# Token pairs for w, output weights four rows per partition, the old state on VectorE and a new order of steps, in a fused linear-attention and gated-MLP kernel

**Chip, cores, metric.** One core of a Trainium2 chip. The metric is device time in microseconds (us), the median of several executions. The kernel before takes 211.56 us (median of 3 runs, 211.44 to 212.03).

## The reference

A linear attention with a decaying state gives x for each token, and a gated MLP with an RMS norm is applied to x. All inputs are float32.

```python
# r, k, v, w: [4 batches, 8 heads, 768 tokens, 48]; u: [8, 48]
for t in range(S):
    cur = einsum('bhd,bhe->bhde', u * k[t], v[t])
    y[t] = einsum('bhd,bhde->bhe', r[t], state + cur)
    state = w[t][..., None] * state + einsum('bhd,bhe->bhde', k[t], v[t])
x = y.transpose(0, 2, 1, 3).reshape(3072, 384)
xn = x / sqrt(mean(x * x) + 1e-6) * rms_g
out = (silu(xn @ w_gate) * (xn @ w_val)) @ w_out     # 384 -> 1536 -> 384
```

## The kernel before

The 768 tokens are cut into 6 superblocks of 128 tokens; a superblock has one chunk per batch, so 4 chunks. Steps are named `step.n.j`, n the superblock, j the chunk or the block of 128 MLP units. One long list, `ORDER`, gives the order of all steps, and each engine executes its own instructions in that order. Loads of r, k, v and w are issued by SyncE, loads of the weights by GpSimd, in between its arithmetic. For a superblock the kernel forms Ln of w, sums it over time with a triangular mask on TensorE, takes the exponentials, multiplies r and k by them, and forms scores, state and y; then the norm, gate, value, `h_mul` and the output matmul. A 512-token superblock has 12 gate and 12 value blocks of three matmuls.

```python
    W_PAIR = ()
    OLD_DVE = ()
...
    def load_w(n, j):                        # one tile [128, 2 * 384] holds two chunks
        ...
        if n in W_PAIR:                      # tokens 2g and 2g+1 in one partition: 384 B runs
            o = t.rearrange("p (h x) -> p h x", h=H)[PD * (j % 2):PD * (j % 2) + PD]
            src = src.rearrange("h (g i) d -> g h (i d)", i=2)
        else:                                # one token per partition: 192 B runs
            o = t.rearrange("p (b h d) -> p b h d", b=2, h=H)[:, j % 2]
            src = src.rearrange("h t d -> t h d")
...
    wg_sb = persist.tile([128, KC, DF], BF16)        # KC = 3, DF = 1536
    wv_sb = persist.tile([128, KC, DF], BF16)
    GV = (0, 4, 12)                                  # two loads each: columns 0-511, 512-1535

    def load_gv(g, h):
        cols = slice(GV[g] * 128, GV[g + 1] * 128)
        dst, s = ((wg_sb, moe_w_gate), (wv_sb, moe_w_val))[h]
        i = nc.gpsimd.dma_start(out=dst[:, :, cols], in_=s[:, cols].rearrange("(c p) f -> p c f", p=128)).ins
        ...
    def load_wo(g, _):                               # FG = 4
        i = nc.gpsimd.dma_start(
            out=wo_sb[:, g * FG:(g + 1) * FG, :],
            in_=moe_w_out[g * FG * 128:(g + 1) * FG * 128, :].rearrange("(c p) m -> p c m", p=128)).ins
...
    def st_mm(n, j):
        ps = bank["st", n, j] = psQ.tile([128, NP, 2 * D], FP32, name="ps_q")
        old = n > 0 and n not in OLD_DVE
        if old:                                      # adds the old state: identity matmul
            nc.tensor.matmul(ps.rearrange("p q x -> p (q x)"), lhsT=ident,
                             rhs=st[:, n % 2, j].rearrange("p q x -> p (q x)"), start=True, stop=False)
        ...
    def st_new(n, j):
        ...
        if n in OLD_DVE:
            nc.vector.tensor_tensor(out=ps, in0=ps, in1=st[:, n % 2, j], op=ALU.add)
        ...
    def fc_mm(ps, ws, n, f):                         # gate and value
        for c in range(KC):
            nc.tensor.matmul(ps, lhsT=ws[:, c, f * 128:(f + 1) * 128], rhs=xnt[n][:, c, :],
                             start=(c == 0), stop=(c == KC - 1))
```

The branches for `W_PAIR` and `OLD_DVE` are there already, with empty lists.

Of the kernel before, what the change touches and what calls it, by code (L numbers as in the profile page):

```python
# [9 lines left out]
FP32 = mybir.dt.float32  # L10
BF16 = mybir.dt.bfloat16
AF = mybir.ActivationFunctionType
# [13 lines left out]
load_w.0.0 load_v.0.0 load_w.0.1 load_k.0.0 load_r.0.0 ln.0.0 load_w.0.2 load_r.0.1 ln.0.1 cs_mm.0.0 load_k.0.1  # L26
cs_mm.0.1 exp_k.0.0 load_w.0.3 exp_r.0.0 k_mul.0.0 bonus_mul.0.0 exp_r.0.1 r_mul.0.0 load_r.0.2 exp_k.0.1 w_tot.0.0
cast_v.0.0 rk_pe.0.0 load_k.0.2 ln.0.2 r_mul.0.1 st_mm.0.0 rk_tr.0.0 cs_mm.0.2 load_w.1.0 st_new.0.0 bonus_mul.0.1
load_v.0.1 q_mm.0.0 k_mul.0.1 ln.0.3 w_tot.0.1 bonus_sum.0.0 rk_pe.0.1 load_k.0.3 exp_k.0.2 q_mask_e.0.0 exp_r.0.2
cs_mm.0.3 bonus_v.0.0 q_mask_o.0.0 rk_tr.0.1 load_r.0.3 k_mul.0.2 y_mm.0.0 bonus_mul.0.2 exp_k.0.3 load_w.1.1  # L30
r_mul.0.2 q_mm.0.1 exp_r.0.3 x_add.0.0 ln.1.0 rk_pe.0.2 load_v.0.2 bonus_sum.0.1 x_sq.0.0 q_mask_e.0.1 cast_v.0.1
load_v.0.3 bonus_v.0.1 w_tot.0.2 rk_tr.0.2 q_mask_o.0.1 cs_mm.1.0 load_w.1.2 k_mul.0.3 bonus_mul.0.3 q_mm.0.2
bonus_sum.0.2 load_k.1.0 r_mul.0.3 ln.1.1 q_mask_o.0.2 rk_pe.0.3 load_w.1.3 x_rstd.0.0 cast_v.0.2 y_mm.0.1 bonus_v.0.2
load_r.1.0 rk_tr.0.3 x_add.0.1 load_gv.0.0 load_r.1.1 q_mask_e.0.2 cast_v.0.3 xn_mul.0.0 load_gv.0.1 bonus_sum.0.3
q_mm.0.3 ln.1.2 bonus_v.0.3 y_mm.0.2 x_sq.0.1 q_mask_e.0.3 st_mm.0.1 exp_k.1.0 load_gv.1.1 w_tot.0.3 x_add.0.2
x_rstd.0.1 cs_mm.1.1 q_mask_o.0.3 exp_r.1.0 load_gv.1.0 x_sq.0.2 y_mm.0.3 exp_k.1.1 load_v.1.0 xn_pe.0.0 x_rstd.0.2
x_add.0.3 st_mm.0.2 st_new.0.1 xn_mul.0.1 x_sq.0.3 st_new.0.2 st_mm.0.3 cs_mm.1.2 x_rstd.0.3 xn_out.0.0 xn_mul.0.2
xn_pe.0.1 xn_mul.0.3 xn_pe.0.2 xn_out.0.1 ln.1.3 xn_pe.0.3 xn_out.0.2 exp_r.1.1 xn_out.0.3 exp_k.1.2 cs_mm.1.3
exp_r.1.2 k_mul.1.0 gate_mm.0.0 st_new.0.3 exp_k.1.3 exp_r.1.3 val_mm.0.0 silu.0.0 gate_mm.0.1 h_mul.0.0 val_mm.0.1
silu.0.1 gate_mm.0.2 h_mul.0.1 load_k.1.1 val_mm.0.2 silu.0.2 gate_mm.0.3 r_mul.1.0 bonus_mul.1.0 val_mm.0.3 silu.0.3  # L40
load_v.1.1 h_mul.0.2 rk_pe.1.0 gate_mm.0.4 h_mul.0.3 load_k.1.2 rk_tr.1.0 r_mul.1.1 val_mm.0.4 load_k.1.3 silu.0.4
bonus_sum.1.0 gate_mm.0.5 cast_v.1.0 h_mul.0.4 load_r.1.2 bonus_v.1.0 val_mm.0.5 silu.0.5 gate_mm.0.6 load_r.1.3
bonus_mul.1.1 h_mul.0.5 val_mm.0.6 k_mul.1.1 silu.0.6 load_w.2.0 gate_mm.0.7 cast_v.1.1 h_mul.0.6 load_v.1.2 st_mm.1.0
load_wo.1.0 k_mul.1.2 silu.0.7 val_mm.0.7 load_w.2.1 st_new.1.0 gate_mm.0.8 bonus_mul.1.2 k_mul.1.3 q_mm.1.0 silu.0.8
rk_pe.1.1 q_mask_e.1.0 val_mm.0.8 rk_tr.1.1 r_mul.1.2 gate_mm.0.9 load_wo.0.0 h_mul.0.7 q_copy_o.1.0 st_mm.1.1
load_wo.2.0 rk_pe.1.2 st_new.1.1 load_k.2.0 val_mm.0.9 rk_tr.1.2 bonus_mul.1.3 r_mul.1.3 q_mm.1.1 gate_mm.0.10
silu.0.9 h_mul.0.8 q_copy_o.1.1 rk_pe.1.3 q_mask_e.1.1 silu.0.10 val_mm.0.10 q_mask_o.1.0 bonus_sum.1.1 rk_tr.1.3
q_mm.1.2 q_mask_o.1.1 gate_mm.0.11 q_mask_e.1.2 q_copy_o.1.2 load_v.1.3 y_mm.1.0 bonus_sum.1.2 silu.0.11 q_mask_o.1.2
x_add.1.0 q_mm.1.3 ln.2.0 bonus_v.1.1 y_mm.1.1 h_mul.0.9 bonus_v.1.2 h_mul.0.10 val_mm.0.11 q_mask_e.1.3 cast_v.1.2
load_r.2.0 cs_mm.2.0 q_copy_o.1.3 h_mul.0.11 y_mm.1.2 x_sq.1.0 load_w.2.2 st_mm.1.2 x_add.1.1 o_mm.0.0 st_new.1.2  # L50
x_rstd.1.0 x_sq.1.1 load_r.2.1 exp_k.2.0 x_rstd.1.1 ln.2.1 load_k.2.1 k_mul.2.0 exp_r.2.0 q_mask_o.1.3 bonus_sum.1.3
o_mm.0.1 cast_v.1.3 load_r.2.2 o_out.0.0 xn_mul.1.0 bonus_v.1.3 w_tot.2.0 x_add.1.2 load_v.2.0 bonus_mul.2.0 x_sq.1.2
y_mm.1.3 load_v.2.1 o_out.0.1 st_mm.1.3 x_add.1.3 ln.2.2 cs_mm.2.1 load_w.2.3 st_new.1.3 o_mm.0.2 x_sq.1.3 x_rstd.1.2
exp_k.2.1 r_mul.2.0 load_k.2.2 xn_mul.1.1 x_rstd.1.3 k_mul.2.1 xn_mul.1.2 bonus_sum.2.0 out_dma.0.0 cs_mm.2.2
exp_r.2.1 cast_v.2.0 o_out.0.2 xn_pe.1.0 xn_pe.1.1 load_r.2.3 r_mul.2.1 bonus_mul.2.1 xn_pe.1.2 xn_mul.1.3 o_mm.0.3
xn_out.1.0 exp_r.2.2 load_k.2.3 xn_out.1.1 ln.2.3 rk_tr.2.0 xn_out.1.2 exp_k.2.2 w_tot.2.1 r_mul.2.2 cast_v.2.1
xn_pe.1.3 cs_mm.2.3 o_out.0.3 bonus_mul.2.2 xn_out.1.3 st_mm.2.0 load_v.2.2 exp_r.2.3 w_tot.2.2 st_mm.2.1 k_mul.2.2
load_k.3.0 exp_k.2.3 gate_mm.1.0 r_mul.2.3 w_tot.2.3 val_mm.1.0 load_r.3.0 silu.1.0 k_mul.2.3 bonus_mul.2.3
gate_mm.1.1 bonus_sum.2.1 rk_tr.2.1 val_mm.1.1 q_mm.2.0 silu.1.1 h_mul.1.0 gate_mm.1.2 load_r.3.1 bonus_v.2.0
h_mul.1.1 load_k.3.1 val_mm.1.2 silu.1.2 q_mask_e.2.0 gate_mm.1.3 h_mul.1.2 rk_tr.2.2 bonus_mul.3.0 val_mm.1.3  # L60
silu.1.3 st_new.2.0 gate_mm.1.4 q_copy_o.2.0 rk_tr.2.3 bonus_sum.2.2 val_mm.1.4 h_mul.1.3 silu.1.4 cast_v.2.2
gate_mm.1.5 h_mul.1.4 load_v.2.3 bonus_v.2.1 val_mm.1.5 st_new.2.1 silu.1.5 load_w.3.0 q_mask_o.2.0 gate_mm.1.6
h_mul.1.5 load_w.3.1 bonus_mul.3.1 val_mm.1.6 q_mm.2.1 load_r.3.2 gate_mm.1.7 q_copy_o.2.1 q_mask_e.2.1 load_k.3.2
st_mm.2.2 silu.1.6 q_mask_o.2.1 val_mm.1.7 silu.1.7 h_mul.1.6 load_k.3.3 y_mm.2.0 h_mul.1.7 gate_mm.1.8 out_dma.0.1
x_add.2.0 val_mm.1.8 st_new.2.2 x_sq.2.0 load_w.3.2 gate_mm.1.9 silu.1.8 x_rstd.2.0 val_mm.1.9 load_w.3.3 silu.1.9
h_mul.1.8 gate_mm.1.10 out_dma.0.2 xn_mul.2.0 h_mul.1.9 q_mm.2.2 load_r.3.3 silu.1.10 bonus_sum.2.3 q_mm.2.3
q_mask_e.2.2 q_copy_o.2.2 val_mm.1.10 load_r.4.0 q_copy_o.2.3 q_mask_o.2.2 gate_mm.1.11 out_dma.0.3 h_mul.1.10
cast_v.2.3 val_mm.1.11 q_mask_e.2.3 silu.1.11 load_k.4.0 q_mask_o.2.3 y_mm.2.1 ln.3.0 h_mul.1.11 bonus_v.2.2 st_mm.2.3
load_r.4.1 y_mm.2.2 x_add.2.1 bonus_v.2.3 o_mm.1.0 load_k.4.1 st_new.2.3 ln.3.1 load_v.3.0 x_add.2.2 x_sq.2.1
bonus_sum.3.0 x_sq.2.2 x_rstd.2.1 bonus_sum.3.1 cs_mm.3.0 xn_pe.2.0 y_mm.2.3 x_rstd.2.2 exp_r.3.0 xn_out.2.0 o_mm.1.1  # L70
xn_mul.2.1 r_mul.3.0 bonus_mul.3.2 exp_k.3.0 x_add.2.3 xn_mul.2.2 o_out.1.0 x_sq.2.3 k_mul.3.0 cs_mm.3.1 ln.3.2
w_tot.3.0 rk_tr.3.0 xn_pe.2.1 x_rstd.2.3 o_mm.1.2 exp_r.3.1 exp_k.3.1 r_mul.3.1 bonus_mul.3.3 ln.3.3 k_mul.3.1
load_k.4.2 o_out.1.1 w_tot.3.1 xn_out.2.1 xn_mul.2.3 load_r.4.2 cs_mm.3.2 bonus_sum.3.2 load_v.3.1 cs_mm.3.3 o_out.1.2
exp_k.3.2 xn_pe.2.2 bonus_mul.4.0 xn_pe.2.3 exp_r.3.2 load_k.4.3 o_mm.1.3 xn_out.2.2 exp_k.3.3 r_mul.3.2 exp_r.3.3
load_r.4.3 xn_out.2.3 w_tot.3.2 k_mul.3.2 load_v.3.2 bonus_mul.4.1 gate_mm.2.0 r_mul.3.3 w_tot.3.3 k_mul.3.3
val_mm.2.0 out_dma.1.0 silu.2.0 gate_mm.2.1 rk_tr.3.1 val_mm.2.1 q_mm.3.0 silu.2.1 h_mul.2.0 load_r.5.0 gate_mm.2.2
q_copy_o.3.0 bonus_sum.3.3 load_k.5.0 val_mm.2.2 h_mul.2.1 silu.2.2 bonus_mul.4.2 load_v.3.3 gate_mm.2.3 h_mul.2.2
rk_tr.3.2 val_mm.2.3 silu.2.3 gate_mm.2.4 h_mul.2.3 bonus_v.3.0 load_w.4.0 val_mm.2.4 q_mask_e.3.0 silu.2.4 rk_tr.3.3
cast_v.3.0 gate_mm.2.5 bonus_sum.4.0 h_mul.2.4 st_mm.3.0 bonus_mul.4.3 silu.2.5 val_mm.2.5 st_new.3.0 load_r.5.1
gate_mm.2.6 load_k.5.1 bonus_sum.4.1 val_mm.2.6 h_mul.2.5 silu.2.6 cast_v.3.1 gate_mm.2.7 load_w.4.1 o_out.1.3  # L80
h_mul.2.6 cast_v.3.2 st_mm.3.1 q_mask_o.3.0 silu.2.7 load_r.5.2 val_mm.2.7 st_new.3.1 bonus_v.3.1 gate_mm.2.8
out_dma.1.1 h_mul.2.7 cast_v.3.3 q_mm.3.1 load_w.4.2 st_mm.3.2 bonus_mul.5.0 q_copy_o.3.1 y_mm.3.0 st_new.3.2 silu.2.8
val_mm.2.8 load_r.5.3 x_add.3.0 gate_mm.2.9 load_k.5.2 q_mask_e.3.1 val_mm.2.9 bonus_v.3.2 load_v.4.0 silu.2.9
bonus_sum.4.2 st_mm.3.3 x_sq.3.0 h_mul.2.8 q_mask_o.3.1 gate_mm.2.10 load_w.4.3 h_mul.2.9 bonus_v.3.3 val_mm.2.10
# [44 lines left out]
def kernel(  # L129
# [46 lines left out]
    CAST_ACT = sel("00 01 02 03 10 11 12 13")  # L176
    EXPR_SB = sel("10 11 12 13")
    EXPK_SB = sel("10 11 12 13")
    W_PAIR = ()
    Q_PAIR = ()  # L180
    OLD_DVE = ()
    XOUT_ACT = sel("")
# [475 lines left out]
```

## Time and profile before

| | before |
|---|---|
| time, median | 211.56 us |
| TensorE busy | 194.5 us, 92% |
| first gate matmul | 29.31 us |
| val of block 1, superblock 1 | 70.56 us |
| from there to the end | 140.9 us |
| gate and value weight loads issued by GpSimd at | 19.32, 20.31, 21.88, 22.68 us |

The page's lines are shown in the prediction (timelines: start, duration, then in brackets the idle time before and what ended it). The first gate block, from the TensorE timeline (start, duration, then in brackets the idle time before and what ended it):

```profile
29.31 0.58 PE L546 MATMUL ps_a<-xnt,wg_sb 128*128 128x512 bf16 x1
30.12 0.63 PE L546 MATMUL ps_a<-xnt,wg_sb 128*128 128x512 bf16 x1 [0.22 <-issue]
```

In all profile lines PE is TensorE (PEld its weight loads), DVE VectorE, ACT ScalarE, POOL GpSimd, SP SyncE; a small q behind a name is the engine issuing something, L546 a line of the kernel, `out<-in` the tiles, x3 the number of instructions, and after q0 and q1 stand packets, MB and the share of the 16 DMA engines. Some matmul records are missing from every trace: this block has three matmuls and two records.

### The profile page before, as it was taken

How to read it: one execution, taken by the hardware profiler on the slowest of the kernel's cores; microseconds unless marked ns; L12 is line 12 of the kernel's file. 1: busy time of each engine (PE TensorE's matmuls, PEld its weight loads, DVE VectorE, ACT ScalarE, POOL GpSimd, SP SyncE). 2: the span in 40 equal slices, each digit the busy share in tenths (PEclk: the TensorE clock that was granted, in tenths of full speed). 3: DMA queues.
4: the chain of work that ended last, by engine and by line, in shares of the span. 5: the costliest groups of instructions: out<-in, count | busy, mean ns of one | idle time of the engine just before them, and what ended most of it. 6: DMA issues, size and time to landing. Idle time of an engine off the chain costs nothing.

```text
span 211.5 us, 4381 instructions
## 1 busy us (share of the span) xinstructions
PE 194.5 (92%) x1534; PEld 107.7 (51%) x1552; DVE 147.6 (70%) x295; ACT 138.1 (65%) x282; POOL 108.6 (51%) x167
## 2 busy tenths in 40 slices
PE   5687779998998799999999999999999999999993
PEld 2455434455664245665455565455655544544563
DVE  6498744899876688988689799667886755235411
ACT  3796994769796356997546998578858873225300
POOL 3498402869597593699697889473222520000000
PEclk9999999999999999999999999999999999999999
DMA  6999999899999999999999999992177030000122
GB/s 131 217 217 183 171 203 211 169 201 168 194 205 188 190 186 228 219 213 192 192 195 222 230 222 124 236 188 48 56 186 127 20 76 20 37 0 37 40 111 76
DMA packets 126878, 32.41 MB, mean 153 GB/s; under 512 B 120580, under 2 KB 126088, under 8 KB 126856
## 3 DMA queue, kind: packets, MB, share of 16 engines
q1 hardware_dynamic: 123664, 28.58, 67.9%
q0 software_dynamic: 3184, 3.54, 10.4%
q8 instruction: 12, 0.20, 0.4%
q14 instruction: 10, 0.08, 0.1%
q10 hardware_dynamic: 8, 0.00, 0.0%
HBM read 25.96 MB, written 4.72 MB: 145 GB/s over the span
## 4 chain that ended last, share of the span: by engine, by line
PE 68%; DMA 7%; SPq 7%; DVE 6%; ACT 5%; issue 3%; POOL 3%; ACTq 0%; DVEq 0%; POOLq 0%
PE ps_b L546 20%; PE ps_a L546 19%; PE ps_q L606 18%; SPq L208 4%; DMA kt<-in_k_dram 3%; DMA vt<-in_v_dram 3%; PE ps_q L443 2%; SPq L221 2%; DMA xnt<-xn 2%; DVE ht L564 2%; PE ps_q L491 2%; PE ps_q L488 1%; DVE rk L402 1%; ACT junk L501 1%; PE ps_b L375 1%
## 5 line engine op out<-in xcount | busy, mean ns | idle before, releaser
L564 DVE TENSOR_TENSOR ht<-ps_b,sg 128x512 bf16<-128x512 f32 x72 | 48.7, 688 | 25.8 <-PE ps_b L546 18.6
L195 ACT ACTIVATE sg<-ps_a 128x512 bf16<-128x512 f32 x72 | 42.6, 596 | 36.3 <-PE ps_a L546 34.9
L546 PE MATMUL ps_b<-xnt,wv_sb 128*128 128x512 bf16 x208 | 58.6, 384 | 2.7 <-DVE rk L402 1.5
L546 PE MATMUL ps_a<-xnt,wg_sb 128*128 128x512 bf16 x206 | 58.8, 385 | 1.2 <-DVE wcol L394 0.6
L606 PE MATMUL ps_q<-wo_sb,ht 128*128 128x384 bf16 (+1 forms) x300 | 49.9, 319 | 0.0
L408 POOL TENSOR_TENSOR ruk<-rt,kt 128x384 f32<-128x384 f32 x24 | 24.3, 1011 | 25.5 <-DMA rt<-in_r_dram 20.2
L606 PEld LDWEIGHTS <-ht 128*128 128x128 bf16 x300 | 28.4, 98 | 16.9
L546 PEld LDWEIGHTS <-wv_sb 128*128 128x128 bf16 x216 | 20.2, 99 | 25.1 <-issue 4.9
L546 PEld LDWEIGHTS <-wg_sb 128*128 128x128 bf16 x216 | 20.2, 99 | 24.2 <-issue 1.7
L409 POOL TENSOR_TENSOR ruk<-ruk,u_bc 128x384 f32<-128x384 f32 x24 | 24.1, 1005 | 1.9
L418 POOL TENSOR_TENSOR ydiag<-vt,diag 128x384 f32<-128x384 f32 x24 | 19.8, 830 | 3.7 <-DVE diag L413 2.9
L461 POOL TENSOR_SCALAR_AFFINE_SELECT qts<-qts 128x512 bf16<-128x512 bf16 x20 | 12.6, 635 | 14.2 <-ACT qts L454 14.2
L450 DVE TENSOR_TENSOR qts<-ps_q,mask_lt 128x512 bf16<-128x512 f32 x24 | 16.2, 683 | 3.8 <-issue 2.5
L496 DVE TENSOR_TENSOR xb<-ps_q,ydiag 128x384 f32<-128x384 f32 x24 | 13.3, 552 | 5.3 <-PE ps_q L491 4.8
L195 ACT ACTIVATE lw<-wt 128x384 bf16<-128x384 f32 x24 | 12.0, 516 | 5.1 <-DMA wt<-in_w_dram 4.9
L514 ACT ACTIVATE xn<-xb,rstd 128x384 bf16<-128x384 f32 x24 | 14.4, 606 | 0.8 <-POOL rstd L510 0.8
L454 ACT CAST qts<-ps_q 128x512 bf16<-128x512 f32 x20 | 11.6, 584 | 4.7 <-PE ps_q L445 4.7
L501 ACT ACTIVATE junk<-xb 128x384 bf16<-128x384 f32 x24 | 12.4, 517 | 3.4 <-DVE xb L496 3.3
L402 DVE TENSOR_TENSOR rk<-kt,ps_b 128x384 bf16<-128x384 f32 x20 | 11.0, 549 | 5.1 <-ACT ps_b L195 3.0
L193 ACT ACT_TABLE_LOAD x10 | 12.8, 1283 | 1.8 <-PEq L642 1.6
L397 DVE TENSOR_TENSOR rk<-rt,ps_a 128x384 bf16<-128x384 f32 x20 | 11.0, 548 | 4.1 <-DMA rt<-in_r_dram 3.0
L615 ACT COPY ob<-ps_q 128x384 f32<-128x384 f32 (+1 forms) x12 | 5.5, 461 | 12.1 <-PE ps_q L606 11.4
(71 smaller groups left out, 271.6 us busy)
## 6 DMA issues: line engine op xcount, KB each, us to landing
wt<-in_w_dram SPq DMA_DIRECT2D x24, 192.0 KB, 3.7
vt<-in_v_dram SPq DMA_DIRECT2D x24, 192.0 KB, 4.2
kt<-in_k_dram SPq DMA_DIRECT2D x24, 192.0 KB, 3.8
rt<-in_r_dram SPq DMA_DIRECT2D x24, 192.0 KB, 3.8
out_dram<-ob SPq DMA_DIRECT2D x23, 192.0 KB, 2.8
wo_sb<-in_moe_w_out_dram POOLq DMA_DIRECT2D x3, 384.0 KB, 6.1
wv_sb<-in_moe_w_val_dram POOLq DMA_DIRECT2D x1, 768.0 KB, 10.6
wg_sb<-in_moe_w_gate_dram POOLq DMA_DIRECT2D x1, 768.0 KB, 14.0
```

What stands on the lines that cost most here:

```text
L195: return nc.scalar.activation(**kw).ins
L402: nc.vector.tensor_tensor(out=rk[:, n % 2, j, 1, :, 0:D], in0=inp["k", n, j], in1=bank["cs_k", n, j][:, 0:DM].rearrange("p (h d) -> p h d" ...
L408: nc.gpsimd.tensor_tensor(out=ruk[n, j], in0=inp["r", n, j], in1=inp["k", n, j], op=ALU.mult)
L409: nc.gpsimd.tensor_tensor(out=ruk[n, j], in0=ruk[n, j], in1=u_bc, op=ALU.mult)
L418: nc.gpsimd.tensor_tensor(out=ydiag[n, j], in0=inp["v", n, j], in1=diag[n, j].to_broadcast([128, H, D]), op=ALU.mult)
L450: nc.vector.tensor_tensor(out=qts[n, j][:, 0], in0=bank["q", n, j][0], in1=bc_mid(mask_lt, NP), op=ALU.mult)
L496: nc.vector.tensor_tensor(out=xb[n, j], in0=bank.pop(("y", n, j)), in1=ydiag[n, j].rearrange("p h d -> p (h d)"), op=ALU.add)
L501: nc.scalar.activation(out=junk, in_=xb[n, j], func=AF.Square, accum_out=rstd[n, j][:, 0:1])
L514: nc.scalar.activation(out=xn, in_=xb[n, j], func=AF.Copy, scale=rstd[n, j][:, 1:2])
L546: nc.tensor.matmul(ps, lhsT=ws[:, c, f * 128:(f + 1) * 128], rhs=xnt[n][:, c, :], start=(c == 0), stop=(c == KC - 1))
L564: nc.vector.tensor_tensor(out=ht[n][:, f, :], in0=bank.pop(("v", n, f)), in1=bank.pop(("sg", n, f)), op=ALU.mult)
L606: nc.tensor.matmul(ps[:, cols], lhsT=ht[n][:, f, b * L:(b + 1) * L], rhs=wo_sb[:, f, cols], start=(f == 0), stop=(f == FC - 1))
```

## The change

The intent is fewer and larger packets for w and for the output weights (in the traces each run of bytes without a gap is one packet: 192 B for one token of w, 384 B for a pair), and twelve matmuls less on TensorE.

```diff
-    W_PAIR = ()
+    W_PAIR = (0, 1)
-    OLD_DVE = ()
+    OLD_DVE = (2, 3, 4)
 ...  # the four pair masks are built on GpSimd after ones_row and i3 instead of before
     def load_wo(g, _):
-            in_=moe_w_out[g * FG * 128:(g + 1) * FG * 128, :].rearrange("(c p) m -> p c m", p=128)).ins
+            in_=moe_w_out[g * FG * 128:(g + 1) * FG * 128, :].rearrange("(p c) m -> p c m", c=FG)).ins
 ...
+    def units(ws, c, f):
+        g = f // FG * FG * 128
+        return ws[:, c, g:g + FG * 128].rearrange("p (m i) -> p i m", i=FG)[:, f % FG, :]
+
     def fc_mm(ps, ws, n, f):
         for c in range(KC):
-            nc.tensor.matmul(ps, lhsT=ws[:, c, f * 128:(f + 1) * 128], rhs=xnt[n][:, c, :],
+            nc.tensor.matmul(ps, lhsT=units(ws, c, f), rhs=xnt[n][:, c, :],
 ...  # the same in fc_half; an unused list ONE_SUM is added
```

With four rows of the output weights in one partition, hidden unit 4p+i lies in partition p, so gate and value must produce their units in that order: `units` reads their weights with a step of four columns. The list of steps was also written anew. The merged steps (`ln` and `cs_mm` of chunks 1 and 3 of superblocks 0 and 1) are dropped, the loads of r and k of superblock 1 and the products for them stand earlier, and the four `load_gv` stand later, behind the first products of superblock 1 on GpSimd.

## The prediction

> **What bounds the kernel now.** I read the page first: busy shares, the slices, then the DMA queues.
>
> ```profile
> PE 194.5 (92%) x1534; PEld 107.7 (51%) x1552; DVE 147.6 (70%) x295; ACT 138.1 (65%) x282; POOL 108.6 (51%) x167
> PE   5687779998998799999999999999999999999993
> DMA  6999999899999999999999999992177030000122
> q1 hardware_dynamic: 123664, 28.58, 67.9%
> q0 software_dynamic: 3184, 3.54, 10.4%
> ```
>
> TensorE is full from slice 14 on (about 70 us) and gappy before; the DMA engines are full from slice 2 to slice 27 (about 143 us). Two regimes, then: up to 70 us the loads set the pace, after it TensorE. The chain of waits confirms where the first ends:
>
> ```profile
> 63.06 0.97 POOL ruk L408
> 64.03 0.09 SPq L208
> 64.17 5.69 DMA kt<-in_k_dram
> ...
> 69.95 0.57 DVE rk L402
> ...
> 70.56 0.81 PE ps_b L546 x3
> ```
>
> That is k of superblock 2, batch 3, the 46th of 96 loads in issue order. Is it late because the engines are full? Summing the trace's DMA records by size: a 192 B packet (the r, k, v and w loads, 1024 each) takes 15.84 ns, so one load is 1024 x 15.84 / 16 = 1.01 us of all engines; the gate and value weights (packets of 1024 and 2048 B on q0) sum to 219 us, 13.7 us; the output weights (1536 packets of 768 B, 85.9 ns) to 132 us, 8.2 us. So 46 x 1.01 + 13.7 + 8.2 + 0.5 (one output store) = 69 us, and the load landed at 69.9. The engines worked without a hole from the start.
>
> How much does TensorE lose to it? The table of windows, and the DVE timeline:
>
> ```profile
> 29.30:51.40 22.10, 21.58 (x153) 10.67 (x154) 16.67 (x30) 15.44 (x24) 12.81 (x15) 1.00 1.07 187
> 51.40:66.20 14.80, 13.99 (x147) 9.25 (x145) 12.68 (x29) 11.66 (x28) 11.90 (x20) 1.00 1.08 207
> 66.20:70.56 4.36, 2.19 (x12) 0.77 (x10) 1.23 (x4) 3.52 (x6) 2.03 (x3) 1.00 1.26 137
> 67.53 0.55 DVE L397 TENSOR_TENSOR rk<-rt,ps_a 128x384 bf16<-128x384 f32 x1 [1.35 <-DMA rt<-in_r_dram]
> 69.95 0.56 DVE L402 TENSOR_TENSOR rk<-kt,ps_b 128x384 bf16<-128x384 f32 x1 [1.80 <-DMA kt<-in_k_dram]
> ```
>
> Columns: window, length, busy time of TensorE, weight loads, DVE, ACT, GpSimd, then clock, DMA share, GB/s. From 66.2 to 70.6 TensorE has 2.2 us of work in 4.4 us. Before that, ACT waited for loads too in 51.4 to 66.2 (1.18 us for v, 1.00 us for w, on the ACT timeline), so some 3.5 us of this stretch could shrink if data came early.
>
> From 70.6 us to the end, 141 us: adding the matmuls at their pitch (three 512-column ones in 0.65 us, twelve 384-column ones in 1.95 us, by the chain) I get 135 us of TensorE work plus 3 us of final store. Only 2 to 3 us of holes are left there.
>
> **What the Trainium skill says.** "DMA: Bandwidth & Descriptors", section "Why small descriptors are slow": each packet carries a fixed overhead, so small descriptors waste the engines. The trace agrees: 4 B packets take 9.0 ns, 192 B 15.8, 512 B 27, 1536 B (uncontended) 62, which is a line of about 9.2 ns + 0.0345 ns per byte. "TensorE: Matmul & The Clock Gate", section "Part 3: Packing small matmuls": matmuls in different row groups run side by side. The trace agrees: the even and odd 48-row q matmuls (L443, L445) start within 0.01 us of each other. The same page, "Weight-path perf modes": fast weight load stays on with a column step of up to 1,024 elements. And "SBUF — State Buffer", the note on cachelines in "Door 1: The DMA port swizzle": 16 B lines, at least two hits per line for full rate; the new step of four bf16 elements is 8 B, two hits. No row of the kernel before has a stepped weight load, so neither of these last two is tested yet.
>
> **The change part by part.**
>
> 1. *w of superblocks 0 and 1 as token pairs.* 8 of 96 loads go from 1024 packets of 192 B to 512 of 384 B. From the line above a 384 B packet is 22.5 ns (estimate). Saved: 8192 x 15.84 - 4096 x 22.5 ns = 129.8 - 92.2 = 37.6 us of engine time, 2.35 us of all 16, all of it before 25 us. ln shrinks from 8 ACT instructions of 0.52 us to 4 of about 0.76 us (an estimate: rows of 384 and 512 columns take 516 and 596 ns, so 384 more columns add 0.24): 1.1 us less ACT. The cumulative sums become 64-row matmuls, twice as many, in two row groups: side by side, so no longer than before (otherwise 16 x 0.16 = 2.6 us more, spread where TensorE isn't the bound). Price: both halves must land before the first ln, the second pair waits for both PSUM banks, and GpSimd builds four more masks (about 3 us by its 0.2 and 0.29 us rows, from 2.7 to 6 us): first sums at 6 us instead of 4.5. Loads, not this, bound the start.
>
> 2. *Output weights 4 rows per partition.* 1536 packets of 768 B become 384 of 3072 B. Sizes 1024 and 2048 B cost 113 and 172 ns on that queue, so 3072 B is 220 to 260 ns: 85 to 99 us instead of 132, or 2.0 to 3.0 us saved of all engines. The window's DMA share of 1.07 says that the two queues overlap somewhat, so I count 1.8 us. Gate and value weights are read with a step of four: 432 weight loads, 98 ns each now, each hidden under a 216 ns matmul. Even at double length they stay hidden: 0.
>
> 3. *Old state on VectorE for superblocks 2 to 4.* 12 matmuls of 384 columns leave (L468, 0.163 us at pitch): 1.95 us, of which 10 fall after 70 us: 1.6 us on the path. Added: 12 DVE additions; rows of this shape take 0.55 us but follow each other at 0.47. That is 1.9 us per superblock on an engine 24.4 busy of 28.2 us (window 70.6 to 98.8), overlapping rows counted twice. It fits, but some h_mul will come later: I charge 0.4 us.
>
> 4. *The new order.* Counting loads: r.1.3 is now 28th instead of 30th, v.0.3 22nd instead of 18th, v.1.2 33rd instead of 32nd, and a cast of v.1.2 now stands before the silu of block 8. By part 1's rates v.0.3 lands at 22 instead of 20.7 us and v.1.2 near 46 us, about when the DVE burst of 46.97 us ends before. The large weight loads stand later on GpSimd (about 22 to 30 us instead of 19 to 23), so gate block 4 can wait. The gates of superblock 0 so end where they do now, 51.4 us, or up to 1.5 us later: I charge 0.5 us. And the first transpose of superblock 2 (1.3 us of all engines: 508 us for 24) is issued ahead of k.2.3; before, it came after.
>
> Sum: k.2.3 lands 2.35 + 1.8 - 1.3 = 2.9 us earlier, at 67 us, and the stretch that could shrink by 3.5 us takes it: -2.9. Then -1.6 + 0.4 on TensorE, +0.5 for the start: **-3.6 us**. I round up a little for the other waits for data that shrink: 207.6 us, 1.9% less. After 70 us the DMA engines are still nearly full, but r and k then run a superblock ahead, so I expect no new wait.
>
> **The rivals.**
>
> *A. The transfers saved aren't on the path.* If ACT and TensorE (14.0 of 14.8 us busy in 51.4 to 66.2) set that stretch, earlier data gives only the 2.2 us hole, or less. For it: TensorE's row is dense there. Against: ACT and DVE waits for loads are listed there. Then about 209.5 us.
>
> *B. VectorE becomes the bound after 70 us.* 26.5 us of its work per superblock by durations, 28.4 with the addition, against 28.2 us per superblock. For: the sum by durations is as long as the period. Against: DVE rows start 0.47 and 0.61 us apart where they last 0.55 and 0.69. Then the 1.6 us is lost and 1 to 2 us added: about 210 us.
>
> *C. Stepped weight loads become visible.* If a load took over 216 ns, the 432 gate and value matmuls would be paced by it; at 300 ns that is 432 x 0.084 = 36 us more. Nothing in the trace speaks for it. I give it 3%.
>
> *D. Data arrives early enough to speed up superblock 0's gates too.* k and r of superblock 1 stand earlier, so the DVE burst at 40 to 49 us is spread out; if v isn't the limit, 2 to 3 us more come off: about 205 us.
>
> **Range and chances.** Main line 207.6, A and B up to 210.5, D down to 204.5: that is the range. The 2% line is 207.3 us, almost at the centre: faster 0.47, same 0.49, slower 0.04 (C, or B and a late start together).
>
> **What would show it.** Right: 384 B packets of about 22 ns and 3072 B ones of 220 to 260; k.2.3 landing near 67 us; val of block 1 of superblock 1 at 67 to 68 instead of 70.6 us; L468 only 4 times; from there to the end about 140 us; gate weight loads under 216 ns. Wrong: gates of superblock 0 ending after 53 us or before 49.5; DVE over 90% in the stages of superblocks 2 and 3 with TensorE gaps ended by it; weight loads over 216 ns; a 384 B packet that costs twice a 192 B one.

## The result and the profile after

The changed kernel takes **223.14 us** (median of 4 runs, 221.77 to 223.44), and the kernel before took 211.5 us (211.44 to 212.03) on the same chip: ratio **1.053**, 95% interval 1.0485 to 1.0579, slower. Ratios here are the mean time of one kernel's fast runs over that of the other's fast runs of the same rounds, so not quite the ratio of the medians quoted. The prediction had 207.6 us and 210.5 at most, so even its direction was wrong.

The page of the changed kernel, busy shares, slices and queues:

```profile
PE 195.6 (88%) x1588; PEld 114.6 (52%) x1588; DVE 153.7 (69%) x307; ACT 138.0 (62%) x278; POOL 112.5 (51%) x177
PE   3586561499999999999999999999999999999994
DMA  6999999999931999899999899990067421000122
q1 hardware_dynamic: 119568, 28.58, 66.4%
q0 software_dynamic: 2032, 3.54, 8.8%
```

A slice is 5.5 us. TensorE's row falls to 1 in slice 7 (about 33 to 39 us) and is full from slice 9 on; the DMA row has a hole in slices 12 and 13. Both queues do carry fewer packets, as intended.

The table of windows of the changed kernel, over the same stretches and with the same columns as in the prediction:

```profile
29.30:51.40 22.10, 12.82 (x85) 6.20 (x86) 9.62 (x18) 8.57 (x17) 8.45 (x10) 1.00 1.11 201
51.40:66.20 14.80, 14.80 (x117) 8.21 (x116) 12.54 (x24) 11.39 (x19) 7.30 (x9) 1.00 0.79 147
66.20:70.56 4.36, 4.34 (x66) 3.20 (x65) 4.26 (x9) 4.35 (x13) 2.79 (x6) 1.00 0.00 0
```

In the first window TensorE works 12.82 us where it worked 21.58. The hole of the last window, which the change was to close, is closed (4.34 busy of 4.36, with no data arriving at all), but only because the work is late: val of block 1 of superblock 1 now starts at 81.25 us instead of 70.56. From there to the end it is 140.5 us (140.9 before). So all of the loss lies earlier. The TensorE timeline of the changed kernel shows where; its last line is that val block:

```profile
34.41 0.61 PE L558 MATMUL ps_a<-xnt,wg_sb 128*128 128x512 bf16 x1 [2.05 <-DMA wg_sb<-in_moe_w_gate_dram]
39.26 1.04 PE L558 MATMUL ps_a<-xnt,wg_sb 128*128 128x512 bf16 x2 [4.23 <-DMA wg_sb<-in_moe_w_gate_dram]
40.09 0.63 PE L558 MATMUL ps_b<-xnt,wv_sb 128*128 128x512 bf16 x1
43.49 1.05 PE L558 MATMUL ps_b<-xnt,wv_sb 128*128 128x512 bf16 x2 [2.77 <-DMA wv_sb<-in_moe_w_val_dram]
...
81.25 0.81 PE L558 MATMUL ps_b<-xnt,wv_sb 128*128 128x512 bf16 x3
```

The first four lines are gate and value of block 0, three matmuls each. The kernel before needed no wait here: its first gate began at 29.31 and ran on. Now the first matmul (rows 0 to 127 of the weights, c=0) goes, and then the second and third (c=1, 2) wait 4.23 us; the value matmuls do the same for 2.77 us. Three matmuls of one block use columns 0 to 511 alone, which one load brings for all three c. A wait *between* c=0 and c=1 cannot be for that load. The chain of waits of the changed kernel names the load:

```profile
17.38 5.54 DMA rt<-in_r_dram
...
23.05 1.00 POOL ruk L416
...
30.36 1.32 POOL ruk L417
31.68 11.77 DMA wv_sb<-in_moe_w_val_dram
...
43.49 1.05 PE ps_b L558 x2
```

The load that landed at 43.45 was issued by GpSimd at 31.68. It is the last of the four, columns 512 to 1535 of the value weights. Block 0 doesn't read one element of it. It was issued that late because it stands behind GpSimd's products for superblock 1, which waited for r.

More readings answer steps of the prediction. By groups of instructions, the gate's weight loads before:

```profile
L546 PEld LDWEIGHTS <-wg_sb 128*128 128x128 bf16 x216 | 20.2, 99 | 24.2 <-issue 1.7 <-DVE wcol L394 1.1 <-DVE xnt L540 0.4
```

and after, with the paired Ln and the addition on VectorE:

```profile
L558 PEld LDWEIGHTS <-wg_sb 128*128 128x128 bf16 x216 | 23.1, 115 | 25.8 <-DMA wg_sb<-in_moe_w_gate_dram 7.0 <-issue 1.1 <-DVE rk L405 0.4
L195 ACT ACTIVATE lw<-wt 128x768 bf16<-128x768 f32 x4 | 3.4, 844 | 6.2 <-DMA wt<-in_w_dram 6.2
L485 DVE TENSOR_TENSOR ps_q<-ps_q,st 128x384 f32<-128x384 f32 x12 | 6.7, 556 | 0.0
```

A stepped weight load takes 115 ns instead of 99, still under the 216 ns of a matmul, so the step costs TensorE nothing by itself (b_wo4_split below confirms it). It is 16% slower, though, than the full rate that the prediction expected of two hits per line. The DMA records by size give a mean of 28.9 ns for a 384 B packet (median 22) and 267 ns for a 3072 B packet. The pairs also touched their neighbours: over the first 23 us the mean of a 192 B packet is 15.5 ns in the kernel before and 18.2 ns in the changed one.

### The profile page after: what moved, and what is told of

Same layout as the page of the kernel before. It is cut to its first block, busy times and chain, and to the rows that moved or that the text cites. A ratio compares the mean times of both kernels' runs of the same rounds, so it can differ in the third digit from the quotient of the medians.

```text
span 221.7 us, 4508 instructions
## 1 busy us (share of the span) xinstructions
PE 195.6 (88%) x1588; PEld 114.6 (52%) x1588; DVE 153.7 (69%) x307; ACT 138.0 (62%) x278; POOL 112.5 (51%) x177
## 4 chain that ended last, share of the span: by engine, by line
PE 67%; DMA 12%; SPq 8%; DVE 3%; POOL 3%; ACT 3%; issue 2%; ACTq 0%; POOLq 0%; DVEq 0%
PE ps_b L558 21%; PE ps_a L558 21%; PE ps_q L618 16%; DMA wv_sb<-in_moe_w_val_dram 5%; SPq L208 5%; DMA rt<-in_r_dram 2%; SPq L221 2%; PE ps_q L451 2%; DMA kt<-in_k_dram 2%; DMA out_dram<-ob 2%; PE ps_q L499 2%; PE ps_q L496 1%; PE ps_q L433 1%; POOL ruk L417 1%; ACT L193 1%
## 5 line engine op out<-in xcount | busy, mean ns | idle before, releaser
L576 DVE TENSOR_TENSOR ht<-ps_b,sg 128x512 bf16<-128x512 f32 x72 | 49.2, 688 | 30.8 <-PE ps_b L558 26.8
L558 PE MATMUL ps_a<-xnt,wg_sb 128*128 128x512 bf16 x216 | 60.8, 391 | 6.5 <-DMA wg_sb<-in_moe_w_gate_dram 6.3
L558 PE MATMUL ps_b<-xnt,wv_sb 128*128 128x512 bf16 x216 | 60.0, 387 | 2.9 <-DMA wv_sb<-in_moe_w_val_dram 2.8
L558 PEld LDWEIGHTS <-wg_sb 128*128 128x128 bf16 x216 | 23.1, 115 | 25.8 <-DMA wg_sb<-in_moe_w_gate_dram 7.0
L558 PEld LDWEIGHTS <-wv_sb 128*128 128x128 bf16 x216 | 23.6, 114 | 24.6 <-DMA wv_sb<-in_moe_w_val_dram 3.7
L417 POOL TENSOR_TENSOR ruk<-ruk,u_bc 128x384 f32<-128x384 f32 x24 | 24.7, 1031 | 1.9
L421 DVE TENSOR_REDUCE diag<-ruk 128x8 f32<-128x384 f32 x24 | 13.0, 544 | 4.3 <-POOL ruk L417 4.3
L195 ACT ACTIVATE lw<-wt 128x384 bf16<-128x384 f32 (+1 forms) x20 | 11.5, 579 | 6.3 <-DMA wt<-in_w_dram 6.2
L625 DVE COPY ob<-ps_q 128x384 f32<-128x384 f32 (+1 forms) x13 | 7.0, 539 | 9.9 <-PE ps_q L618 9.9
L487 DVE TENSOR_TENSOR st<-ps_q,wcol 48x192 bf16<-48x192 f32 x32 | 11.4, 355 | 2.6 <-PE ps_q L479 2.0
```

Source lines behind the costliest of these rows:

```text
L195: return nc.scalar.activation(**kw).ins
L417: nc.gpsimd.tensor_tensor(out=ruk[n, j], in0=ruk[n, j], in1=u_bc, op=ALU.mult)
L421: nc.vector.tensor_reduce(out=diag[n, j].rearrange("p h o -> p (h o)"), in_=ruk[n, j], axis=mybir.AxisListType.X, op=ALU.add)
L558: nc.tensor.matmul(ps, lhsT=units(ws, c, f), rhs=xnt[n][:, c, :], start=(c == 0), stop=(c == KC - 1))
L576: nc.vector.tensor_tensor(out=ht[n][:, f, :], in0=bank.pop(("v", n, f)), in1=bank.pop(("sg", n, f)), op=ALU.mult)
```

## The experiments

**Theory:** the compiler's dependency tracking makes a stepped read of chunk c=1 or 2 wait for the neighbouring load too (a *false wait*), and in the new order that load is issued late. **Rivals:** the late issue alone; the output store at the head of SyncE's queue (SyncE issues nothing from 57.3 to 70.5 us, and the DMA row has its hole there); the token pairs; the old state on VectorE; the new order as a whole.

### gv_early

The changed kernel with the four weight loads issued earlier, at 21.8 to 24.4 us.

```diff
 ORDER: ... bonus_v.0.1
+  load_gv.0.0 load_gv.0.1 load_gv.1.0 load_gv.1.1
 ...    (removed from their later places)
```

> The changed kernel with one thing moved: the four loads of gate and value weights are issued on GpSimd right after the second bonus_v of superblock 0 (about 21 us), not behind the bonus products of superblock 1. Theory 1 (the weights arrive late, because the in-order GpSimd queue waits for r and k of superblock 1 first): the three TensorE waits for weights (2.05 + 4.23 + 2.77 = 9.05 us) go, first gate matmul near 31 us instead of 34.4, gates of superblock 0 over near 54 instead of 65 us, time 209 to 214 us. Theory 2 (the SP queue stuck behind the first output store is what costs): no more than 3 us better, above 219. Theory 3 (the three parts themselves cost): above 217.

Measured: 219.83 us (219.34 to 220.63), before on the same chip 213.25; ratio 1.031 (1.0272 to 1.0355). The TensorE timeline:

```profile
34.19 0.59 PE L558 MATMUL ps_a<-xnt,wg_sb 128*128 128x512 bf16 x1 [0.74 <-DVE xnt L544]
35.60 0.63 PE L558 MATMUL ps_a<-xnt,wg_sb 128*128 128x512 bf16 x1 [0.82 <-DMA wg_sb<-in_moe_w_gate_dram]
36.03 0.63 PE L558 MATMUL ps_b<-xnt,wv_sb 128*128 128x512 bf16 x1
40.33 1.04 PE L558 MATMUL ps_b<-xnt,wv_sb 128*128 128x512 bf16 x2 [3.67 <-DMA wv_sb<-in_moe_w_val_dram]
```

The first gate is no earlier, since it now waits for its input, and the value block still waits 3.67 us between its first and second matmul. My theory 1 had 209 to 214 us and no such waits: the issue time is a part of the cost, not the whole.

### a_out

The changed kernel with the first output store moved behind the last load of k of superblock 2, so that it cannot block SyncE's queue.

```diff
 ORDER: ... load_k.2.3
+  out_dma.0.0
```

> The changed kernel with only the first output store moved in the SP order, from ahead of the loads k.2.2, r.2.3, k.2.3 to behind k.2.3. Theory 2 (SP stands still from 57 to 70 us behind that store, with the DMA engines idle, and k.2.3 lands at 75.8): 5 us or more better, below 218 us. Theory 1 (late weights set it; after them TensorE has its own backlog up to 80 us): within 2 us of the changed kernel, 221 to 224 us.

Measured: 223.74 us (223.08 to 223.99), ratio 1.049. No gain: with the store out of the way SyncE stands from 60.9 to 70.4 us at its next entry, a transpose of superblock 2 that waits 9.5 us for VectorE's product. The hole is a consequence of late work, and this rival falls.

### b_all

All three parts, in the order of the kernel before (merged steps dropped, four steps moved where a pair needs it).

> All three parts of the change, but in the order of the kernel before (ln and sums of the odd batches dropped, four steps moved where the shared PSUM tiles demand it). Theory 1 (the order's late weights cost, the parts do not): 206 to 211 us. Theory 3 (stepped weight loads, 64-row sums or the VectorE additions cost): above 215 us.

Measured: 224.02 us (223.52 to 225.48), ratio 1.050 (1.046 to 1.0535). My expectation missed by far: the old order does not save the change. The first gate's first matmul went at 34.96 us and the second waited 6.57 us for the gate weights. So the wait sits in the parts, not in the order.

### b_gv_late

The kernel before with its weight loads issued late, contiguous reads untouched: the first product of superblock 1 stands earlier on GpSimd, the first two loads (in swapped order) behind it, and the other two follow as before. All four issue at 27.7 to 30.2 us.

```diff
 ORDER: ... exp_k.1.0
+  bonus_mul.1.0 load_gv.0.1 load_gv.0.0
   load_gv.1.1
 ...    (the three moved steps are removed from their old places)
```

> The kernel before with only the weight loads moved late: the first bonus product of superblock 1 stands before them on GpSimd, so they issue at about 26 to 29 us instead of 19 to 23. Theory 1: TensorE waits for the weights, first gate matmul near 34 us, 215 to 219 us. Theories 2 and 3: 211 to 212 us, nothing else changed.

Measured: 218.27 us (217.06 to 218.69), ratio 1.023 (1.0183 to 1.0273). The timeline:

```profile
37.18 0.61 PE L546 MATMUL ps_a<-xnt,wg_sb 128*128 128x512 bf16 x1 [6.76 <-DMA wg_sb<-in_moe_w_gate_dram]
38.01 0.63 PE L546 MATMUL ps_a<-xnt,wg_sb 128*128 128x512 bf16 x1 [0.22 <-issue]
...
45.73 0.82 PE L546 MATMUL ps_a<-xnt,wg_sb 128*128 128x512 bf16 x3 [1.41 <-DMA wg_sb<-in_moe_w_gate_dram]
```

With contiguous reads TensorE waits before the first matmul, runs gate and value of blocks 0 to 3 without a wait, and waits again before block 4, the first block that needs the second load. That is what waits on the data itself look like. Late issue costs something in its own right (2.3%; the interval lies clear of 1), but it does not split a block.

### b_wo4 and b_wo4_split

The decisive pair: the kernel before, its order untouched, with nothing but the output weights four rows per partition and the stepped reads; then the same with the gate and value weights each in two tiles, one per load.

```diff
-    wg_sb = persist.tile([128, KC, DF], BF16)
-    wv_sb = persist.tile([128, KC, DF], BF16)
+    wg_sb = (persist.tile([128, KC, 512], BF16, name="wga"), persist.tile([128, KC, DF - 512], BF16, name="wgb"))
+    wv_sb = (persist.tile([128, KC, 512], BF16, name="wva"), persist.tile([128, KC, DF - 512], BF16, name="wvb"))
 ...
-        i = nc.gpsimd.dma_start(out=dst[:, :, cols], in_=...
+        i = nc.gpsimd.dma_start(out=dst[g], in_=...
 ...  # units() picks the tile by the group's first column
```

> The kernel before, its order untouched, with the output-weight part alone: 4 rows per partition and stepped reads of gate and value weights. New theory (false wait: a stepped read of columns 0 to 511 makes chunks 1 and 2 of the very first gate and value block wait for the second pair of weight loads, columns 512 to 1535, which it does not use): the first gate matmul starts near 29.3 us, its second waits until the second pair has landed, near 36 to 37 us; time 215 to 219 us. Rival (stepped reads are slow in themselves): weight loads over 216 ns and matmuls over 0.65 us for three all through. Rival (this part is harmless, the order and the pairs cost): 209 to 212 us.

> The same part alone, with the gate and value weights each in two tiles, one per load, so that a stepped read can meet only its own load. Same steps, same instructions, same transfers. False wait: no wait inside the first gate block, time 209 to 212 us. Slow stepped reads: as the one-tile version.

Measured: b_wo4 219.39 us (219.03 to 219.92), ratio 1.036 (1.0303 to 1.0423); b_wo4_split 211.44 us (211.21 to 214.86), ratio 0.998 (0.9927 to 1.0038), before on that chip 211.62. The timelines, one tile first, with the second gate load (columns 512 to 1535) from the chain of waits:

```profile
23.02 14.01 DMA wg_sb<-in_moe_w_gate_dram
29.53 0.59 PE L550 MATMUL ps_a<-xnt,wg_sb 128*128 128x512 bf16 x1
37.49 0.63 PE L550 MATMUL ps_a<-xnt,wg_sb 128*128 128x512 bf16 x1 [7.37 <-DMA wg_sb<-in_moe_w_gate_dram]
37.92 1.49 PE L550 MATMUL ps_b<-xnt,wv_sb 128*128 128x512 bf16 x3
```

and two tiles:

```profile
33.17 0.59 PE L551 MATMUL ps_a<-xnt,wga 128*128 128x512 bf16 x1
33.98 0.63 PE L551 MATMUL ps_a<-xnt,wga 128*128 128x512 bf16 x1 [0.22 <-issue]
34.41 1.49 PE L551 MATMUL ps_b<-xnt,wva 128*128 128x512 bf16 x3
```

The profiled run of b_wo4_split was a slow one (over 1.5% above the fastest run of the same kernel), so only its order of waits is read from it; its times are those of the fast runs. The same loads, the same stepped reads, the same arithmetic: with one tile TensorE waits 7.37 us inside the first block, until the second load has landed at 37.03 (the record of the matmul between the two shown is missing; its weights too were loaded only at 37.08). With two tiles it does not wait, though the second load lands only at 37.1 there, issued at 23.0 and 14.1 us under way. The wait is false, and it costs 3.8% of the time alone (1.036 against 0.998). Where the rule lies was not read from the compiler. The pattern (c=0 free, c=1 and 2 waiting) fits a comparison of address ranges from first to last element: the second load's range runs from column 512 of c=0 to column 1535 of c=2, the gaps included, and the stepped reads of c=1 and 2 lie inside that range while that of c=0 doesn't. A contiguous read of c=1 or 2 lies in that range too and did not wait (b_gv_late), so it would have to be compared more finely. This rule is a guess that fits; no run tests it.

### a_split and a_split_gv

The changed kernel with the two tiles, and the same with the early weight loads of gv_early as well.

> The changed kernel with the weights in two tiles each and nothing else. The first pair still lands near 34 us and the second near 43, so blocks 0 to 3 of superblock 0 (5.2 us of TensorE) run in what was a wait, and block 4 waits for the rest. False wait as a cause beside late weights: 217 to 220 us. Not a cause: 222 to 224 us.

> The changed kernel with both: two tiles per weight and the weight loads issued early (about 21 to 24 us). If false wait and late weights are the whole of the loss: 211 to 215 us, no wait for weights over 2 us. If the parts cost by themselves: above 217 us.

Measured: a_split 215.04 us (214.0 to 215.2), ratio 1.0146 (1.0093 to 1.0199); a_split_gv 215.16 us (214.69 to 218.04), ratio 1.0155 (1.0097 to 1.0212; its 218.04 us is a slow run). In the timeline of a_split:

```profile
34.20 0.61 PE L559 MATMUL ps_a<-xnt,wga 128*128 128x512 bf16 x1 [2.07 <-DMA wga<-in_moe_w_gate_dram]
35.04 0.63 PE L559 MATMUL ps_a<-xnt,wga 128*128 128x512 bf16 x1 [0.22 <-issue]
```

The waits inside block 0 are gone, and with them some 8 us (1.053 to 1.015). With two tiles the early issue adds nothing: it took 2% off the changed kernel only because it shortened the false wait. What is left, 1.5%, is another matter.

### b_w_pair, b_old_dve, b_wo4_old_split and b_all_split

Each remaining part alone in the order of the kernel before, then the output weights with two tiles and the old state, then all three with two tiles. Edits: `W_PAIR = (0, 1)` with its merged steps; `OLD_DVE = (2, 3, 4)`; combinations of these with the edits above.

> The kernel before with the token pairs of superblocks 0 and 1 alone, in its own order of steps (the merged steps dropped, four steps moved where the pairs need it), contiguous weights, old state on TensorE. Theory 1 (the token pairs cost the remaining 1.5% of the changed kernel with two weight tiles: packets of 384 B at 28.9 ns against twice 15.8 are hardly cheaper, the sums of 64 rows and the later masks delay superblock 0): first gate later than 31 us and 213.5 to 216 us, ratio 1.01 to 1.02. Theory 2 (the pairs are neutral and the rest is the new order of steps): 210.5 to 212.5 us, first gate within 1 us of 29.3. Theory 3 (the pairs help as I predicted, by 2.9 us): 208 to 209.5 us.

> The kernel before with the old state of superblocks 2 to 4 added on VectorE, nothing else, order unchanged. My prediction's part 3: TensorE loses 12 matmuls of 0.16 us net and gains nothing, 1.6 us at most, VectorE gains 12 adds of 0.56 us: 210 to 211.5 us, ratio 0.992 to 1.000. Rival (the longer way from the score matmul to the state, through VectorE, holds up the next chunk): 212 to 214 us, ratio 1.003 to 1.012, with waits of TensorE on the state grown.

> The kernel before with output weights of 4 rows per partition and stepped reads, gate and value weights in two tiles each, and the old state of superblocks 2 to 4 on VectorE; no pairs, order unchanged. If the costs and gains add: the ratio of the run with split tiles (0.998) times what the old state alone gives (0.992 to 1.000): 210 to 211.5 us. If the shorter output load (384 packets of 3072 B at 267 ns, 102 us of queue time against 132 us for 1536 of 768 B) frees anything that the old state can use, under 209.5 us, and this would be the version that beats both kernels.

> All three parts in the order of the kernel before, gate and value weights in two tiles each. The same three parts with one tile gave ratio 1.050; the false wait there was 6.6 us on TensorE, so without it 215 to 217 us by that number, 1.014 to 1.025, if the pairs bear the rest (theory 1), and equal within 1% to the changed kernel with two tiles in its own order (1.0146). If the new order bears the rest (theory 2), this kernel comes to 209 to 212 us.

Measured, before on the same chip 212.97 us (211.43 to 216.41, 11 runs, two of them slow, as is one run of b_wo4_old_split):

| kernel | us | ratio | 95% interval |
|---|---|---|---|
| b_w_pair | 214.97 | 1.009 | 1.0038 to 1.0138 |
| b_old_dve | 214.80 | 1.006 | 1.0005 to 1.0117 |
| b_wo4_old_split | 213.87 | 1.002 | 0.9966 to 1.0076 |
| b_all_split | 216.94 | 1.0185 | 1.0141 to 1.0229 |

No part is worth anything in this order, nor are the output weights and the old state together. The pairs cost about 1%: the first Ln, which now needs two loads, begins at 6.42 us instead of 3.92, the first sums at 7.31 instead of 4.50, and the first gate matmul comes at 34.12. That last figure must be read with care: the kernel before itself shows 29.31, but b_wo4_split and b_old_dve, which change nothing before it, show 33.17 and 32.45 (both waited for a load of w that took 11.0 and 10.1 us), so a single first-gate time is uncertain by 3 to 4 us. The old state alone saves nothing here, and costs if anything (the interval just excludes 1): TensorE's waits for the product of `h_mul` grow. First the kernel before, then b_old_dve, from the list of waits (total us, times, longest):

```profile
PE ps_b L546 <- DVE ht L564: 0.7, 2, 0.4
```

```profile
PE ps_b L546 <- DVE ht L564: 2.5, 5, 0.9
```

### a_pair1_split, a_split_no_old and b_wo4_pair1_split

The changed kernel with two tiles and pairs in superblock 1 only; the same with pairs in both but the old state back on TensorE; and the kernel before with the output weights, two tiles, and pairs in superblock 1 only.

```diff
-    W_PAIR = (0, 1)
+    W_PAIR = (1,)          # a_pair1_split, b_wo4_pair1_split
-    OLD_DVE = (2, 3, 4)
+    OLD_DVE = ()           # a_split_no_old, b_wo4_pair1_split
```

> The changed kernel with two tiles for each of the gate and value weights, and the token pairs of superblock 1 only; w of superblock 0 by single rows, its Ln and sums next to where the pair's stood in the order. Theory 1 (the late start of superblock 0 is what remains): first Ln near 4 us instead of 6.4, first gate matmul at 30 to 32.5 us instead of 34.2, and 211 to 213 us on a chip where the kernel before takes 211.6 (ratio 0.998 to 1.006, down from 1.0146). Theory 2 (the start is not what sets the end; the loads that come later do): the first gate comes earlier but TensorE waits longer after it, ratio 1.012 to 1.018.

> The changed kernel with two tiles for each of the gate and value weights and the old state back on TensorE in all superblocks. Prediction's part 3 (VectorE's add saves TensorE 1.6 us at most): ratio 1.015 to 1.022, slower than the run with split tiles (1.0146). Rival from the run with the old state alone (1.006 of before, waits of TensorE on VectorE's products up from 0.7 to 2.5 us): ratio 1.005 to 1.012.

> The kernel before in its own order with output weights of 4 rows per partition and stepped reads on two tiles each, and token pairs in superblock 1 only (old state on TensorE). If the pairs' saving of load time is worth something once they don't delay the start: 4 loads of 512 packets of 384 B instead of 1024 of 192 B save 4 x (1024 x 15.84 - 512 x 28.9) ns / 16 = 0.36 us, so hardly: ratio 0.99 to 1.00. If the later Ln and the sums of 64 rows cost in superblock 1 too: 1.002 to 1.01.

Measured, before on the same chip 211.24 us (210.01 to 213.51, 11 runs): a_pair1_split 213.63 us, ratio 1.0115 (1.0079 to 1.015); a_split_no_old 215.64 us, ratio 1.0205 (1.0166 to 1.0244); b_wo4_pair1_split 215.63 us, ratio 1.0206 (1.0169 to 1.0243). On a_pair1_split theory 1 fell, and theory 2's range was missed by a hair: it took off 0.3% where I expected some 1% or nothing, and the first gate still came at 33.23. In the new order the old state on VectorE seems to save 0.6% (1.0205 against a_split's 1.0146, intervals overlapping), as part 3 of the prediction had it; in the old order it does not. The third kernel was badly built, and says nothing of pairs as such. Its ScalarE timeline:

```profile
18.04 0.84 ACT L196 ACTIVATE lw<-wt 128x768 bf16<-128x768 f32 x1 [4.05 <-DMA wt<-in_w_dram]
```

I left the Ln of the pair where the Ln of the first chunk alone had stood. There it waits 4.05 us for the second chunk's load and holds up everything behind it on ScalarE.

### a_no_pair_split and a_order_split

The changed kernel with two tiles and no pairs at all; then with none of the three parts, so that only the order of steps (and the two tiles) is new.

```diff
-    W_PAIR = (0, 1)
+    W_PAIR = ()            # both; ln and cs_mm of the odd chunks behind those of the even ones
-    OLD_DVE = (2, 3, 4)
+    OLD_DVE = ()           # a_order_split, with the old output-weights layout and contiguous reads
```

> The changed kernel with two tiles for each of the gate and value weights and no token pairs at all (single rows, Ln and sums next to where the pair's stood). Theory 1 (the pairs bear the rest, superblock 1's too): ratio 0.994 to 1.005. Theory 2 (the new order bears the rest): ratio 1.008 to 1.016, no better than the kernel with pairs in superblock 1 only (1.0115).

> Only the order of steps of the changed kernel, with none of the three parts, two weight tiles, contiguous reads. The old state alone was worth 0.6% in this order and the output weights nothing, so by sums 0.6% above the kernel without pairs: under theory 1 ratio 1.000 to 1.011, under theory 2 ratio 1.014 to 1.022. First gate matmul at 33 us or later under theory 2.

Measured, before on the same chip 211.15 us (12 runs): a_no_pair_split 213.75 us (212.2 to 215.24), ratio 1.0134 (1.0092 to 1.0177); a_order_split 215.25 us (213.67 to 215.78), ratio 1.0175 (1.0134 to 1.0216). Theory 2 holds: the new order alone costs as much as the whole remainder, and the pairs are neutral in it (1.0134 without them, 1.0146 with). But the costs do not add: in the old order the three parts cost 1.85% with two tiles (b_all_split), in the new order nothing beyond the order's own. The TensorE timeline of a_order_split:

```profile
34.34 0.61 PE L559 MATMUL ps_a<-xnt,wga 128*128 128x512 bf16 x1 [2.97 <-DMA wga<-in_moe_w_gate_dram]
```

Its gate weights were issued at 25.64 us (19.32 before), and the first gate waits for them. But a_split_gv took that wait away with pairs in place and won nothing, so what in the order costs the 1.75% stays open. One caveat: the Ln and sums of the odd chunks were put back at places of my choice, which may cost a little too.

No kernel tried beats the kernel before beyond the error; b_wo4_split equals it.

## Why the prediction was wrong

**The failed step** is in part 2: "Gate and value weights are read with a step of four ... Even at double length they stay hidden: 0." The length was right (115 ns, hidden). What failed is the silent assumption that a different way of reading a tile changes only the duration of the read. It changed the *set of loads that the read waits for*: 7.37 us of wait in the old order, 3.8% of the time, shown by b_wo4 against b_wo4_split; in the changed kernel 38 of the 53 thousandths (1.053 to 1.015, a_split). The prediction's own sign of a wrong course appeared too: the gates of superblock 0 end at 65.8 us, not by 53. Rival C looked at stepped reads too, and asked only whether they are slower.

**Part 4, order: mis-sized.** I charged 0.5 us for late weight loads, taking it that only gate block 4 can wait for the second pair. By a_order_split the order costs 1.75%, some 3.7 us. Late issue also fed the false wait: gv_early took back 1.053 to 1.031. I had the issue times right (22 to 30 us predicted, 25 to 32 measured) and read no consequence from them, because I took each load to be needed where its columns are first used.

**Part 1, pairs: mis-sized, and a cost left out.** Half of the 384 B packets do take what was estimated (median 22 ns, estimate 22.5), but many take longer, and the mean is 28.9. By the mean the saving is 8192 x 15.84 - 4096 x 28.9 ns = 11.4 us of engine time, 0.7 us of all 16 engines instead of 2.35. And the 14552 packets of 192 B that move in the same first 23 us take 2.7 ns more each, some 39 us of engine time, more than was saved. The new order without pairs (a_no_pair_split) has 15.6 ns there, and the pairs in the old order (b_w_pair) 18.8, so this comes with the pairs. Why is open: each paired load fills 64 of the 128 partitions, and no run varied that. The paired Ln takes 0.84 us instead of 0.76. The price was put at sums 1.5 us later; in b_w_pair they begin 2.8 us later. The net was not -2.35 us but +1% in the old order and about zero in the new.

**Part 2, output weights: right in the packets.** 3072 B packets take 267 ns, just over the estimate of 220 to 260: 384 x 267 = 103 us instead of 132, 1.8 us of all engines, as counted. It is worth no time that can be seen (0.998): rival A, that the saved transfers aren't on the path, was the better view of it.

**Part 3, old state: right size, in one order only.** Four of the 16 identity matmuls remain; the addition takes 0.556 us. In the new order it seems to save about 0.6% (1.3 us against 1.2 net predicted), without the intervals parting; in the old one it costs 0.6% at the edge of the error, with longer waits for `h_mul` in the one profile, a mild form of rival B.

**Slips in the working.** The transpose of superblock 2 was charged 1.3 us, the mean of 24. But 16 of them (r and k) move 1024 packets of 256 B and 8 (x) move 384; at 26.1 ns a packet the first kind takes 1.7 us of all engines, so the 2.9 us should have been 2.5. TensorE's row is full from slice 15, not 14. Neither bears on the miss.

**What of the dense part?** The hole at 66 to 70 us did close. From the first gate to the end the kernel before needs 182.2 us (211.5 - 29.3). The changed kernel needs 180.3 without the two waits inside block 0 (221.7 - 34.4 - 7.0), and a_split, which has no such waits, 178.1 (212.3 - 34.2). So after the first gate these single profiles show a gain of up to 4 us, about the predicted size. It was spent on starting the gates 5 us later, and the 7.0 us of false waits came on top. That it has about the predicted size is luck as far as the runs show, and no merit of the parts: b_gv_late, which has none of them and only starts later, also has 178.1 by the same sum (216.7 - 37.2 - 1.4). Probably late work finds its data ready; no run tests it. And a first gate that can lie 3 to 4 us off from run to run makes all four sums rough.

## What to carry to other kernels

When a change alters *how* a tile is read (step, view, rearrangement), ask which writers of that tile the read will now wait for, and look in the trace for a wait in the middle of a group that uses one load's data: that is the mark of a false wait, and one tile per load removes it. Issue times of loads must be checked against the reads that are made to wait for them, not those that need them. And an earlier gain can be real and yet invisible: compare stages, from a fixed event to a fixed event, before saying that it did not come.

## What the Trainium skill lacked or had wrong

- Dependencies between a stepped operand and a load of neighbouring columns of the same tile: none of the pages read has it. Cost here: 7.37 us of TensorE wait in b_wo4, none with one tile per load (1.036 against 0.998).
- "TensorE: Matmul & The Clock Gate", section "Weight-path perf modes": the page lets fast weight load stay on with a stepped column, and a step of four bf16 elements cost little here: 99 ns contiguous, 115 ns stepped, all hidden under the matmuls. The 16% is not on the page.
- "DMA: Bandwidth & Descriptors", section "Why small descriptors are slow": a fixed overhead per packet fits the undisturbed packets (median 15 ns for 192 B, 22 ns for 384 B). What the page lacks is what happened under full load: the mean for 384 B is 28.9 ns, only 9% less per byte than 2 x 15.84, where the line in the prediction promised 29%, and the 192 B packets beside them went from 15.5 to 18.2 ns.
